# Agent attention followed by a maxout feed-forward on one core: w_out loaded after the first hosted group's keys and values, and the first batch's linear product copied out of PSUM by VectorE

## The chip, the core and the metric

The kernel runs on 1 core of one Trainium2 chip. The metric is the device time of one execution in microseconds (us). Each kernel is run several times, and the median is given. A profiled execution gives the trace, in which every instruction has its start and its duration. The engines are named PE (TensorE), DVE (VectorE), ACT (ScalarE), POOL (GpSimd) and SP (SyncE, which here only issues DMAs).

## What is computed

```
scale = 1 / sqrt(128)
sm(a, b)  = softmax over the last axis of scale * (a @ b^T)
agent_v   = sm(agents, k) @ v              # per batch: 49 agents x 128
x         = sm(q, agents) @ agent_v        # per batch: 12544 rows x 128
h         = max(x @ w1, x @ w2, x @ w3)    # 768 wide
out       = h @ w_out                      # 50176 rows x 128
```

There are B = 4 batches of 12544 rows, 49 agents and 128 channels, all in float32. The three weights are 128 x 768 and w_out is 768 x 128.

## The kernel before

**Algebra.** The rows of x are mixtures of 49 agent rows, so the kernel multiplies agent_v with the weights once per batch and gets a small matrix G (tile `G`, bf16). A query tile is then worked on from its 49 exponentials e alone (tile `e_q`). The maximum over three products is written as w1's product plus a maximum of differences: x@w1 + max(0, x@(w2-w1), x@(w3-w1)). The columns of `wall` are therefore the differences w2-w1 (from C21) and w3-w1 (from C31), and behind them (from C1O) the *linear part*, w1 @ w_out, 128 columns wide. For one of the six blocks of 128 hidden columns (number FI = 3) the differences are formed in another way, and its two steps accumulate in one tile. The reciprocal of the sum of e (tile `recips`) is applied at the end, in `out_scale`.

**Ramp.** The keys and values of batch 0 are handled first, in 12 groups. SP loads keys and values (L315, tiles `st`), POOL casts the keys (L320, `k_bf`), PE transposes them (L334, `uv_ps`), DVE copies the result to SBUF (L340, `kT`), PE multiplies with the agents (L352), ACT takes exponentials (L357, `e_k`), PE multiplies them with the values (L363), and DVE adds up (L375, `Vacc`). At the end DVE normalises (L442, L443, `avT`), and PE and DVE form batch 0's G from `wall` in pieces (L456; L471, L477, L478 and L482 copy out of PSUM).

**Linear part of batch 0.** It depends on w_out, which is loaded late. `load_w_out` (L233) puts the load into SP's queue, and `prep_w_out` (L262) casts it on POOL to `wo_bf`. PE multiplies it with the transposed w1 in six steps (`prep_linear1`, L276) into the PSUM tile `o_ps`. `linear_out` (L280) copies 128 columns of that into `wall`. `linear_product` (L285) multiplies them with `avT` into another part of the same PSUM tile, and `linear_product_out` (L289) copies 256 columns into G's last columns. `out_linear` (L620) is the first reader of those.

**Steady part.** The queries are handled in 49 groups of 8 tiles of 128 rows (`q_group`, s = 0 to 48). POOL casts (L538, `q_bf`). PE transposes (L543) and DVE copies out (L549, `qT`; for group 0 ACT does it, L551); later groups use a transposing DMA instead (L558). PE forms the scores (L564) and ACT the exponentials (L570, `e_q`). Then for each of the six hidden blocks: PE forms both differences (L590, `uv_ps`), ACT applies the relu to one of them (L605, `a_sb`) and DVE takes the maximum with the other (L615, `r`). For block FI ACT does both steps (L602, L613). PE multiplies with w_out (L629, `o_ps`), DVE scales (L642, `o_sb`) and SP stores (L649). The sums of e are L578, their reciprocals L584. While the queries of one batch are handled, the keys and values of the next one are handled beside them, one group in each query group (*hosted* groups; for the first two the keys are transposed by PE, for the others by DMA, L336). At a batch border the totals are formed (L435, L445) and G of the next batch (L456, L463).

**Order of the work.** Nothing is scheduled by a compiler. Each step is entered with a key, `at(key, fn, name, needs, ring, frees)`, and `emit` sorts by the key, holding a step back until the steps that it needs are entered and its ring of PSUM buffers has a free one. The rings are "uv" with 3 buffers, "om" with 2, and "a" with 3 (this one in SBUF). Each engine then works on its own instructions in that order, and waits for others by semaphores. The keys come from tables (`KEY`, `BEGIN` and others); one query group is 6.0 long. `KEY["u0"]` is -0.804, so `last_key`, the key of batch 0's last key group, is -2.804. Loads go into a ring of 14 tiles. SP's DMAs take eight semaphores in turn, and one is issued only when the DMA eight before it has landed.

The steps of the diff were entered like this:

```
at(key, linear_out, "linear_out", [("linear", f) for f in range(NF)])   # key = 6 + KEY["a0"] + 0.01
at(key + 0.4, linear_product, "lin_b", ["linear_out"])
at(6 + KEY["a1"] + 0.01, linear_product_out, "lin_c", ["lin_b", ("normalise", 0)])
at(last_key - 29.85, load_w_out)
at(last_key - 3.24, prep_w_out)
```

Among SP's loads this places w_out behind the load of query group 0 and ahead of the keys and values of hosted group 0.

Of the kernel before, what the change touches and what calls it, by code (L numbers as in the profile page):

```python
# [11 lines left out]
AF = mybir.ActivationFunctionType  # L12
# [4 lines left out]
def kernel(  # L17
# [18 lines left out]
    nc = tc.nc  # L36
    B, N, C = q.shape
# [121 lines left out]
    def at(key, fn, name=None, needs=(), ring=None, frees=()):  # L159

        ops.append((key, len(ops), fn, name, needs, ring, frees))
# [76 lines left out]
    C21, C31, C1O = 0, Dff, 2 * Dff  # L240
    wall = const.tile([P, 2 * Dff + 3 * C], BF16, name="wall")
    nc.vector.memset(wall[:, C1O:], 0.0)
    WC = 2 * Dff + 2 * C
# [26 lines left out]
    linear = {}  # L270
# [4 lines left out]
    def prep_linear1(f):  # L275
        nc.tensor.matmul(linear["t"][:, :C], w1T[:, f, :], wo_bf[:, f, :], start=(f == 0),  # L276
                         stop=(f == NF - 1))

    def linear_out():
        nc.scalar.activation(wall[:, C1O + C:C1O + 2 * C], linear["t"][:, :C], AF.Copy)  # L280

    def linear_product():
        for h in range(2):
# [2 lines left out]
                             start=False, stop=True, skip_group_check=True)  # L286

    def linear_product_out():
        nc.scalar.activation(G[0][:, C1O:WC], linear["t"][:, C:3 * C], AF.Copy)  # L289

    def keep_busy(times):
        t = small_tile("m_ps")
# [4 lines left out]
    G = {}  # L297
# [410 lines left out]
    def ramp():  # L708

        at(KEY["lin1"] - 6, linear_tile, "linear", ["lin_a"], "om", ["lin_c"])  # L710
        keys = sorted(KEY[f"oc1{f}"] for f in range(NF))
        for f, key in enumerate(keys):
            at(key - 6, lambda f=f: prep_linear1(f), ("linear", f), ["linear"])
        key = 6 + KEY["a0"] + 0.01
        at(key, linear_out, "linear_out", [("linear", f) for f in range(NF)])
        at(key + 0.4, linear_product, "lin_b", ["linear_out"])
        at(6 + KEY["a1"] + 0.01, linear_product_out, "lin_c", ["lin_b", ("normalise", 0)])

# [1 line left out]
    last_key = KEY["u0"] - 2  # L722
# [3 lines left out]
    at(first_key - 6.5, load_weights)  # L726
    at(first_key + 30.2, prep_weights)
    at(first_key + 37.1, prep_linear0, "lin_a", (), "om", ["lin_a"])
    at(last_key - 29.85, load_w_out)
    at(last_key - 3.24, prep_w_out)  # L730
    fillers = []
    for g, n in enumerate(first_sizes):
        k_group(0, sum(first_sizes[:g]), n, first_key + 6.0 * g, None)
# [16 lines left out]
    for s in range(NQ):  # L750
        q_group(s)
    ramp()

    with tc.manual_schedule():
# [31 lines left out]
```

## Time and profile before

| | |
|---|---|
| time, median of 5 runs | 461.55 us (461.52 to 461.67) |
| the profiled execution: its own time | 461.54 us |
| its span, first to last instruction | 459.7 us |
| TensorE clock granted | 0.999 of full speed |
| busy PE / DVE / ACT / POOL | 95% / 87% / 87% / 37% of the span |

A time in the trace is counted from the span's start. A line of the timeline gives start, duration, engine, source line, operation, the tiles (written <- read), their shape, and in brackets how long the engine had stood idle before and what ended that. A line of the chain gives start, duration and what the chain passed through. "issue" there is time in which the engine waited for nothing that the profile shows, and a q behind an engine's name stands for its sequencer, the part that reads instructions and waits for semaphores.

### The profile page before, as it was taken

The page shows a single profiled execution, that of the slowest core. Times are in us where ns is not written, and L with a number is a line of the kernel's source. Part 1 is how long each engine was busy: PE and PEld are TensorE (multiplying, and loading weights), DVE is VectorE, ACT ScalarE, POOL GpSimd, SP SyncE. Part 2 cuts the span into 40 slices and gives each one's busy share as a digit, 9 for nine tenths or more (in the row PEclk, how much of TensorE's full clock was granted, in tenths as well). Part 3 has the DMA queues.
Part 4 walks back from the last instruction along what each step waited for, and adds up shares of the span by engine and source line. Part 5 has one row for each costly group of instructions (what it writes and reads, how often), then busy time and mean ns, then how long its engine had stood idle before and what let it go on. Part 6 is the DMA issues. An engine that isn't in the chain of part 4 may idle for free.

```text
span 459.7 us, 13330 instructions
## 1 busy us (share of the span) xinstructions
PE 436.7 (95%) x5462; PEld 274.0 (60%) x5462; DVE 401.7 (87%) x510; ACT 397.8 (87%) x464; POOL 171.3 (37%) x179
## 2 busy tenths in 40 slices
PE   2598999999999999999999999999999999999996
PEld 2465456666656666666656666666656555555554
DVE  3256899999989999999989999999988999999995
ACT  3365989899899899898999998998999999998993
POOL 2234964644362535535272446354150100100000
PEclk9999999999999999999999999999999999999999
DMA  8999999999999899997998999996856556553212
GB/s 315 409 411 390 356 343 354 334 344 266 305 305 310 282 282 311 298 270 226 243 358 298 279 295 334 278 269 193 179 115 186 159 169 179 159 140 96 89 69 116
DMA packets 82632, 118.53 MB, mean 258 GB/s; under 512 B 56391, under 2 KB 57867, under 8 KB 82571
## 3 DMA queue, kind: packets, MB, share of 16 engines
q1 hardware_dynamic: 82368, 117.59, 84.7%
q8 instruction: 42, 0.69, 0.6%
q14 instruction: 19, 0.16, 0.1%
q10 hardware_dynamic: 203, 0.10, 0.1%
HBM read 78.74 MB, written 25.69 MB: 227 GB/s over the span
## 4 chain that ended last, share of the span: by engine, by line
PE 81%; DMA 9%; DVE 3%; ACT 3%; issue 1%; SPq 1%; POOL 0%; ACTq 0%; POOLq 0%; DVEq 0%
PE uv_ps L590 35%; PE o_ps L629 30%; DMA st<-in_k_dram 7%; PE o_ps L620 6%; PE m_ps L543 4%; PE m_ps L564 3%; DVE r L615 3%; ACT a_sb L605 2%; DMA st<-in_v_dram 2%; PE m_ps L363 2%; PE m_ps L352 1%; PE m_ps L578 1%; SPq L315 1%; ACT e_q L570 0%; ACT G L463 0%
## 5 line engine op out<-in xcount | busy, mean ns | idle before, releaser
L615 DVE TENSOR_TENSOR r<-uv_ps,a_sb 128x1024 bf16<-128x1024 f32 x245 | 297.4, 1220 | 16.5 <-PE uv_ps L590 7.8
L605 ACT ACTIVATE a_sb<-uv_ps 128x1024 bf16<-128x1024 f32 x245 | 241.2, 1028 | 13.7 <-PE uv_ps L590 12.3
L590 PE MATMUL uv_ps<-e_q,G 49*128 49x512 bf16 (+3 forms) x1248 | 186.7, 368 | 1.8 <-ACT a_sb L605 0.4
L629 PE MATMUL o_ps<-wo_bf,r 128*128 128x128 bf16 x2352 | 175.4, 220 | 0.0
L629 PEld LDWEIGHTS <-r 128*128 128x128 bf16 x2352 | 137.7, 98 | 40.6 <-issue 39.0
L590 PEld LDWEIGHTS <-G 49*128 49x128 bf16 x1248 | 58.1, 93 | 64.0 <-issue 32.1
L382 POOL TENSOR_TENSOR Eacc<-Eacc,e_k 128x441 f32<-128x441 f32 (+1 forms) x30 | 30.4, 1015 | 124.5 <-ACT e_k L357 124.5
L642 DVE TENSOR_TENSOR o_sb<-o_ps,recips 128x512 f32<-128x512 f32 x97 | 66.8, 689 | 8.4 <-PE o_ps L629 5.6
L538 POOL CAST q_bf<-st 128x1024 bf16<-128x1024 f32 x49 | 50.9, 1040 | 62.2 <-DMA qT<-q_bf 59.2
L613 ACT ACTIVATE r<-uv_ps 128x1024 bf16<-128x1024 f32 x49 | 50.2, 1024 | 19.6 <-PE uv_ps L590 19.3
L320 POOL CAST k_bf<-st 128x1152 bf16<-128x1152 f32 (+2 forms) x45 | 50.2, 1117 | 29.2 <-DMA st<-in_k_dram 27.4
L602 ACT ACTIVATE uv_ps<-uv_ps 128x1024 f32<-128x1024 f32 x49 | 49.7, 1013 | 0.3
L620 PE MATMUL o_ps<-G,e_q 128*128 128x256 bf16 x196 | 38.0, 276 | 0.0
L327 POOL CAST v_bf<-st 128x1152 bf16<-128x1152 f32 (+1 forms) x33 | 37.4, 1134 | 0.6 <-PE m_ps L352 0.3
L570 ACT ACTIVATE e_q<-m_ps 128x512 bf16<-128x512 f32 x49 | 29.9, 610 | 0.5 <-PE m_ps L564 0.5
L325 ACT ACTIVATE v_bf<-st 128x1152 bf16<-128x1152 f32 (+1 forms) x12 | 12.9, 1074 | 14.2 <-DMA st<-in_v_dram 14.1
L340 DVE COPY kT<-uv_ps 128x1152 bf16<-128x1152 bf16 (+1 forms) x14 | 9.9, 710 | 15.2 <-PE uv_ps L334 15.2
L620 PEld LDWEIGHTS <-e_q 128*128 128x128 bf16 x196 | 12.5, 97 | 17.9 <-issue 17.3
L543 PEld LDWEIGHTS <-q_bf 128*128 128x128 bf16 x264 | 14.9, 98 | 13.0 <-issue 10.6
L549 DVE COPY qT<-m_ps 128x1024 bf16<-128x1024 bf16 x32 | 21.8, 681 | 0.1
L543 PE MATMUL m_ps<-ident,q_bf 128*128 128x128 bf16 x264 | 20.4, 220 | 0.3 <-POOL q_bf L538 0.3
L334 PE MATMUL uv_ps<-ident,k_bf 128*128 128x128 bf16 x116 | 11.2, 255 | 9.4 <-POOL k_bf L320 8.4
(75 smaller groups left out, 236.6 us busy)
## 6 DMA issues: line engine op xcount, KB each, us to landing
st<-in_q_dram SPq DMA_DIRECT2D x46, 512.0 KB, 4.8
out_dram<-o_sb SPq DMA_DIRECT2D x46, 512.0 KB, 3.7
st<-in_k_dram SPq DMA_DIRECT2D x40, 576.0 KB, 6.8
st<-in_v_dram SPq DMA_DIRECT2D x40, 576.0 KB, 8.3
st<-in_k_dram SPq DMA_DIRECT2D x3, 512.0 KB, 7.2
st<-in_v_dram SPq DMA_DIRECT2D x3, 512.0 KB, 7.9
wst<-in_moe_w_dram SPq DMA_DIRECT2D x3, 384.0 KB, 10.4
st<-in_q_dram SPq DMA_DIRECT2D x2, 384.0 KB, 4.8
```

Source lines behind the costliest of these rows:

```text
L320: nc.gpsimd.tensor_copy(out=d["kb"][:, :n, :], in_=d["k"][:, :n, :])
L327: nc.gpsimd.tensor_copy(out=d["vb"][:, :n, :], in_=d["v"][:, :n, :])
L538: nc.gpsimd.tensor_copy(out=d["qb"], in_=d["q"])
L543: nc.tensor.transpose(t[:, j * P:(j + 1) * P], d["qb"][:, j, :], ident)
L590: nc.tensor.matmul(t[:, h, j0 * P:j1 * P], G[b][h * H:h * H + A, col + f * P:col + (f + 1) * P], d["e"][h * H:h * H + A, j0 * P:j1 * P], s ...
L602: nc.scalar.activation(u, u, AF.Relu)
L605: nc.scalar.activation(a_sb[f], u, AF.Relu)
L613: nc.scalar.activation(r, v_ps[f], AF.Relu)
L615: nc.vector.tensor_tensor(out=r, in0=v_ps[f], in1=a_sb[f], op=ALU.max)
L620: nc.tensor.matmul(t[:, i * 2 * C:(i + 1) * 2 * C], d["e"][:, jj * P:(jj + 1) * P], G[batch[jj]][:, C1O:C1O + 2 * C], start=(i == 0), stop ...
L629: nc.tensor.matmul(t[:, c:c + C], r_sb[f][:, h, jj * P:(jj + 1) * P], wo_bf[:, f, :], start=False, stop=True, skip_group_check=True)
L642: nc.vector.tensor_tensor(out=d["out"][:, j:j + m, :], in0=d["o", o].rearrange("p (j c) -> p j c", c=C), in1=d["r"][:, j:j + m].unsqueeze( ...
```

## The change

`load_w_out` gets the key -24.55, just behind the load of hosted group 0 (-24.6). In SP's queue w_out now stands behind that group's keys and values and ahead of query group 1. `prep_w_out` gets the key -6.084 instead of -6.044. On POOL the cast of w_out now stands ahead of the cast of query group 1 instead of behind it. `linear_out` and `linear_product_out` are copies by DVE instead of ACT, and the second has another key: on DVE the first stands behind the last two `r` of query group 0 and ahead of a reciprocal (L584) and an addition to `Vacc` (L375), the second behind these two and ahead of the first `r` of query group 1. PE's order is the same.

```diff
     def linear_out():
-        nc.scalar.activation(wall[:, C1O + C:C1O + 2 * C], linear["t"][:, :C], AF.Copy)
+        nc.vector.tensor_copy(out=wall[:, C1O + C:C1O + 2 * C], in_=linear["t"][:, :C])
...
     def linear_product_out():
-        nc.scalar.activation(G[0][:, C1O:WC], linear["t"][:, C:3 * C], AF.Copy)
+        nc.vector.tensor_copy(out=G[0][:, C1O:WC], in_=linear["t"][:, C:3 * C])
...
-        at(6 + KEY["a1"] + 0.01, linear_product_out, "lin_c", ["lin_b", ("normalise", 0)])
+        at(6 + KEY["ka"] + 0.01, linear_product_out, "lin_c", ["lin_b", ("normalise", 0)])
...
-    at(last_key - 29.85, load_w_out)
-    at(last_key - 3.24, prep_w_out)
+    at(-24.55, load_w_out)
+    at(last_key - 3.28, prep_w_out)
```

## The prediction, made before the changed kernel ran

> **What bounds the kernel now.** I read the page's chain first: by engine it is almost all TensorE (PE), the rest a DMA part and small pieces of VectorE (DVE) and ScalarE (ACT). Then the chain of waits cut to the first 70 us, where everything that the diff touches runs.
>
> ```profile
> PE 81%; DMA 9%; DVE 3%; ACT 3%; issue 1%; SPq 1%; POOL 0%; ACTq 0%; POOLq 0%; DVEq 0%
> 35.22 8.38 DMA st<-in_k_dram
> 43.75 1.16 POOL k_bf L320
> 44.95 0.68 PE uv_ps L334 x9
> ...
> 54.31 1.02 ACT a_sb L605
> 55.34 0.18 ACT wall L280
> 55.52 0.04 issue
> 55.56 0.30 PE o_ps L285 x2
> ...
> 61.33 0.04 issue
> 61.37 0.39 PE uv_ps L590 x2
> ```
>
> Until 43.6 us the chain is loads; the last is the keys of batch 1's group 0, cast by GpSimd (POOL) and turned by PE. It passes both moved evacuations (L280; L289 follows 1 us later) and leaves ACT at 61.37. From there PE runs without a gap up to the batch borders, and since PE's instructions keep their order, what the first 61 us gain or lose is carried to the end. So the sum is made there. Next, the engines by time:
>
> ```profile
> 43.75 1.15 POOL L320 CAST k_bf<-st 128x1152 bf16<-128x1152 f32 x1 [2.02 <-DMA st<-in_k_dram]
> 45.18 1.15 POOL L327 CAST v_bf<-st 128x1152 bf16<-128x1152 f32 x1 [0.28 <-DMA st<-in_v_dram]
> 46.41 1.04 POOL L538 CAST q_bf<-st 128x1024 bf16<-128x1024 f32 x1
> 47.39 0.83 POOL L262 CAST wo_bf<-wo_st 128x768 bf16<-128x768 f32 x1
> ...
> 51.88 3.49 DVE L615 TENSOR_TENSOR r<-uv_ps,a_sb 128x1024 bf16<-128x1024 f32 x3
> 56.29 0.41 ACT L289 ACTIVATE G<-o_ps 128x256 bf16<-128x256 f32 x1
> 58.46 1.02 ACT L613 ACTIVATE r<-uv_ps 128x1024 bf16<-128x1024 f32 x1 [0.85 <-PE uv_ps L590]
> ```
>
> POOL stands 2.02 us before k_bf, and PE 0.91 before L334 because of it. DVE is full when L280's input is ready.
>
> **Part 1: w_out behind group 0's keys and values.** SP issues load n when load n-8 has landed, so the issues (1.43 us apart per 576 KB) show the landings. Group 0's query load lands at 40.65 (it releases the issue at 40.70), w_out at 41.85 (issued 33.75, 8.1 to landing), the keys at 43.60, the values at 45.03, group 1's query (q1) at 46.36. Bytes and order beyond these three loads do not change: keys 1.25 earlier at 42.35, values at 43.8, w_out at 45.03, q1 still at 46.36.
>
> POOL: k_bf runs 42.50 to 43.65. PE is free at 44.04 (44.95 less 0.91), so L334 starts 0.91 earlier and the rest of the 1.25 is lost to PE's own work. What is late next: the first hidden product (u0, L590) waits for DVE's second 512-column copy of G (L478, ends 44.90), so it starts at 44.95 instead of 45.56, 0.61 earlier. Its a_sb and the fourth L590 pair, which waits for that a_sb, move by 0.61 too, and PE would reach the turn of q1 (L543, now 47.83) at 47.22. But q1's cast cannot start before 46.41, as now: it ends at 47.45, and the turn comes at 47.50 (0.05 from POOL's end to PE, as at 44.90 to 44.95). **Gain 0.33**, not 1.25. The steps behind it follow one another with no slack of their own: qT (L549), the r at 49.10, the turn at 50.38 that waits for that r, the a_sb and e_q up to 54.31, the three r up to 55.37. All move by 0.33.
>
> The cast of w_out now stands before q1's on POOL: 45.1 to 45.9, in the time in which POOL waits for q1. That cover is 0.45; beyond it each us that w_out lands later is a us on q1's cast. Its reader on PE (L276, 52.80) does not notice. On SP the load passes two others and waits one lane later; the issues before and after stand as they are. The next key and value casts (48.16, 49.31) wait for loads landing at 47.73 and 49.17, and L334's second turn waits for the r anyway: nothing.
>
> **Part 2: two evacuations from ACT to DVE.** L280 on DVE (128x128, fp32 to bf16) is not in the trace. Nearest rows: CAST 128x512 0.69 and 128x256 0.42 (L477, L471), so about 0.29; bounds 0.20 (COPY 128x49, L378) and 0.42. L289 is 128x256: 0.42 against ACT's 0.41. On the path: the third r ends at 55.04 (55.37 less 0.33) and stands before L280 in the queue; L276 is done by then. L280 ends about 55.30 and L285 starts at 55.35 instead of 55.56: of the 0.33 only 0.21 is left here. Behind L280 wait the reciprocal and Vacc (0.36 together, no early readers). L289 waits for L285's end (55.65) and ends at 56.10, before L620 (56.57). Behind it stands the r at 56.29, whose input PE gives at 55.97: 0.1 late at most, with 0.25 of slack before its PE reader.
>
> ACT loses 0.18 and 0.27 of its row (starts 55.23 to 55.39 and 56.29 to 56.56). L602 then waits for PE alone: 56.18 to 57.20, where it ended at 57.62 and held back the L590 pair at 57.67 by 0.12. That pair comes at 57.34, so 0.33 stands again.
>
> [...]
>
> **Part 3: the stall on ACT, and how the instruction count moves it.** L613 at 58.46 starts 0.40 after the end of its matmul pair (58.06). At the second border a DVE r shows the same, with its sequencer already released:
>
> ```profile
> 239.29 0.02 DVEq L615
> 239.31 0.40 issue
> 239.70 1.24 DVE r L615
> ...
> 350.65 0.02 DVEq L615
> 350.68 0.04 issue
> 350.72 1.24 DVE r L615
> q14 instruction: 19, 0.16, 0.1%
> ```
>
> The last line is a DMA queue: packets, MB, share. 0.40 against 0.04. Counted in the trace, semaphore instructions included, the stalled ones are ACT's 64th, DVE's 448th (and 192nd, at 110.99, 0.35 idle), POOL's 69th (68.32, 0.42): for DVE 256 apart, and ACT's place modulo 128 is the same. About 3 us after each, queue q14 moves a packet of 8 KB. I read it as a step in the instruction supply that stops an engine's sequencer for 0.35 at each 128th instruction, and is seen only when nothing is queued behind it. In the built program ACT has one instruction less before L613 (two copies out, one semaphore wait in) and DVE two more. So the stop falls on the a_sb behind L613, under L613's 1.02 us. L613 then starts at 57.83: 58.46 less 0.33 less 0.30. The a_sb pair (1.95 long, 0.92 behind) ends at 60.70, and PE's wait at 61.37 ends at 60.74. **Gain at 61 us: 0.63.**
>
> Later stops: DVE's 192nd falls under an r instead (the six L590 at 112.86 took 0.92 where others take 0.78: 0.14 back), the 448th too (238.85 to 242.50 took 3.65 where the first border's like stretch, 137.52 to 141.01, took 3.49: 0.16 back). Against it DVE's stop at 174.9 shows for some 0.05, and ACT's at 446.47 delays an a_sb by 0.17 and the L590 pair behind L602 by 0.14. Net 0.11 back, taken as 0.12.
>
> [...]
>
> **Sum.** 0.33 + 0.30 + 0.12 = 0.75 off the profiled execution's 461.54 (span 459.7, 1.8 around it): 460.79; off the median 461.55: **460.8 us**.
>
> **Rivals.**
> *A, the stops stay where they are:* 0.33 alone, 461.2. For it: three or four events are few to count by. Against: the distances fit.
> *B, q1 is not the bound:* if q1's load landed 0.3 sooner (the slowest three of a load's 16 parts come some 1.1 after the others, and their lag moves by 0.3 at 43.3), PE's own 0.61 would pass: 0.61 + 0.30 + 0.12, 460.5. For it: that lag. Against: q1 has the same bytes before it.
> *C, slower: w_out blocks POOL.* Place: w_out's cast ahead of q1's. It lands 8.1 after issue now; the same size in wst took 10.4. Issued at 36.70 it would land at 47.1, q1's cast would end at 48.96 and the turn start 1.19 late; with 0.42 back from the stops that is 462.3, and from 10.6 on (462.5) it is slower. Against it: SP's order and equal bytes put it at 45.03.
> *D, nothing moves:* the keys' gain is eaten by u0's wait for G and L280's by DVE's queue; 461.5. Against it: 0.61 of slack at u0.
>
> **How the numbers follow.** A measurement of this kernel tells about 0.2%, 0.92 us, from no change: faster is below 460.63. The forecast 0.50, B 0.25, A 0.15, D 0.05, C 0.05. The forecast's own spread is 0.25 (0.1 for L280's bounds, the rest landing times), so some 0.16 of its half lies below 460.63; of B 0.23. Together faster 0.40, same 0.55, slower 0.05. The range goes from B less 0.2 (460.3) to A plus 0.2 (461.4).
>
> **What would show it.** Right: k_bf at about 42.5, wo_bf at 45.1 before q_bf at 46.41, L543 at 47.50, L280 on DVE at about 55.0, L613 at 57.8 without the extra 0.35, the L590 behind the a_sb pair at 60.7, no 0.40 "issue" near 239. Wrong: q_bf later than 46.5 (C), L543 near 47.2 (B), L613 still 0.4 behind its matmuls (A), or a shift after 61 us that grows or shrinks by more than 0.2 outside those stops.

## The result, and the profile after

The changed kernel takes **460.68 us** (median of 23 runs, 460.53 to 461.10) where the kernel before takes 461.58 (43 runs in the same comparison, 461.32 to 462.01). The ratio is 0.998, with a 95% interval of 0.9974 to 0.9985: 0.90 us less. The interval excludes 1, though 460.68 is just above the 460.63 that I had set as the border of a measurable gain. The forecast was 460.8, from a sum of 0.75.

The profiled execution of after is one of its slowest, 461.08 us with a span of 459.295, so the two traces differ by 0.45 only. I return to that below. First the chain of waits of after, in the ramp and up to PE's wait at 61 us (start, duration, what the chain passed through):

```profile
37.49 9.34 DMA st<-in_q_dram
...
46.88 1.05 POOL q_bf L538
...
47.98 0.64 PE m_ps L543 x8
...
55.50 0.21 DVE wall L280
...
55.75 0.30 PE o_ps L285 x2
...
58.22 0.39 ACT r L613
...
59.14 1.94 ACT a_sb L605 x2
...
61.13 0.39 PE uv_ps L590 x2
```

The last load on the chain is now q1's, not the keys of group 0, and L280 stands on it as a DVE piece. PE's pair behind the a_sb starts at 61.13 where it was 61.37, although the turn of q1 starts later than before (47.98 for 47.83). The next lines are POOL's part of the timeline, and then DVE's and ACT's around the moved copies (start, duration, engine, line, operation, tiles, shapes, idle time before it and its releaser):

```profile
43.02 1.15 POOL L320 CAST k_bf<-st 128x1152 bf16<-128x1152 f32 x1 [1.18 <-PE m_ps L294]
...
45.56 0.83 POOL L262 CAST wo_bf<-wo_st 128x768 bf16<-128x768 f32 x1
46.88 1.04 POOL L538 CAST q_bf<-st 128x1024 bf16<-128x1024 f32 x1 [0.49 <-DMA st<-in_q_dram]
```

```profile
55.41 0.28 DVE L280 CAST wall<-o_ps 128x128 bf16<-128x128 f32 x1
56.09 0.42 DVE L289 CAST G<-o_ps 128x256 bf16<-128x256 f32 x1 [0.20 <-PE o_ps L285]
56.63 1.01 ACT L602 ACTIVATE uv_ps<-uv_ps 128x1024 f32<-128x1024 f32 x1 [0.22 <-PE uv_ps L590]
58.22 1.02 ACT L613 ACTIVATE r<-uv_ps 128x1024 bf16<-128x1024 f32 x1 [0.58 <-PE uv_ps L590]
```

POOL has done w_out's cast 0.49 before q1 lands, so that cast is hidden, and q1's cast waits for its DMA. L602 now waits for PE (0.22) and no longer for ACT's own copies. L613's bracket says 0.58 where it said 0.85. Its sequencer is released at 58.16, so 0.06 is left of the 0.37 that lay between the release (58.09) and the start before.

The later places where I expected a shift, in the chain of after (L590 at the second hidden stretch, the second border, and the last groups):

```profile
112.62 0.77 PE uv_ps L590 x6
...
238.46 0.39 PE uv_ps L590 x2
238.85 0.78 PE o_ps L629 x12
...
447.55 0.88 PE uv_ps L590 x6
```

In the chain of before, the six L590 ahead of L613 and the six at 112 read:

```profile
57.39 0.90 PE uv_ps L590 x6
...
112.86 0.92 PE uv_ps L590 x6
```

The six at 112 take 0.77 now, the 0.40 of "issue" at the border is gone, and the six at 447 took 0.75 before (448.11 0.75): two gains and a loss, each where it was forecast.

### The profile page after: what moved, and what is told of

The parts are those of the page before. It is cut to its first block, busy times and chain, and to the rows that moved or that the text cites. A ratio compares the mean times of both kernels' runs of the same rounds, so it can differ in the third digit from the quotient of the medians.

```text
span 459.3 us, 13331 instructions
## 1 busy us (share of the span) xinstructions
PE 437.0 (95%) x5462; PEld 274.7 (60%) x5462; DVE 402.2 (88%) x512; ACT 397.0 (86%) x462; POOL 171.5 (37%) x179
## 4 chain that ended last, share of the span: by engine, by line
PE 81%; DMA 10%; DVE 4%; ACT 3%; issue 1%; POOL 0%; ACTq 0%; SPq 0%; DVEq 0%
PE uv_ps L590 34%; PE o_ps L629 30%; PE o_ps L620 6%; DMA st<-in_k_dram 5%; PE m_ps L543 4%; DVE r L615 4%; PE m_ps L564 3%; DMA st<-in_v_dram 2%; DMA st<-in_q_dram 2%; ACT a_sb L605 2%; PE m_ps L363 2%; PE m_ps L352 1%; DMA ag_st<-in_agents_dram 1%; PE m_ps L578 1%; ACT G L463 0%
## 5 line engine op out<-in xcount | busy, mean ns | idle before, releaser
L590 PE MATMUL uv_ps<-e_q,G 49*128 49x512 bf16 (+3 forms) x1248 | 186.3, 368 | 1.7 <-DVE G L478 0.2
L590 PEld LDWEIGHTS <-G 49*128 49x128 bf16 x1248 | 58.1, 93 | 63.8 <-issue 31.3
L613 ACT ACTIVATE r<-uv_ps 128x1024 bf16<-128x1024 f32 x49 | 50.2, 1024 | 19.3 <-PE uv_ps L590 19.1
L602 ACT ACTIVATE uv_ps<-uv_ps 128x1024 f32<-128x1024 f32 x49 | 49.6, 1012 | 0.4 <-PE uv_ps L590 0.2
L543 PEld LDWEIGHTS <-q_bf 128*128 128x128 bf16 x264 | 14.8, 98 | 13.6 <-issue 11.1
L543 PE MATMUL m_ps<-ident,q_bf 128*128 128x128 bf16 x264 | 20.4, 220 | 0.7 <-POOL q_bf L538 0.7
L564 PE MATMUL m_ps<-qT,agT 128*64 128x512 bf16 (+3 forms) x104 | 19.9, 388 | 0.0
```

The source lines that it names most:

```text
L543: nc.tensor.transpose(t[:, j * P:(j + 1) * P], d["qb"][:, j, :], ident)
L590: nc.tensor.matmul(t[:, h, j0 * P:j1 * P], G[b][h * H:h * H + A, col + f * P:col + (f + 1) * P], d["e"][h * H:h * H + A, j0 * P:j1 * P], s ...
L602: nc.scalar.activation(u, u, AF.Relu)
L613: nc.scalar.activation(r, v_ps[f], AF.Relu)
```

## The experiments

**The base.** All further kernels start from one in which the 47 DMA transposes are plain copies. Its edit:

```
-  nc.sync.dma_start_transpose(out=d["kT"][:, :n, :], ...      # L336
+  nc.sync.dma_start(out=d["kT"][:, :n, :], ...
-  nc.sync.dma_start_transpose(out=d["qT"], ...                # L558
+  nc.sync.dma_start(out=d["qT"], ...
```

> Before, with its 47 DMA transposes (L336, L558: k tiles from batch 1's group 2 on, q tiles of the late groups) replaced by plain DMA copies of the same tiles, so that those tiles go on untransposed; every compute engine's instructions are the same and in the same order. All further kernels here are built on this base. Both theories: the first 61 us as in before (L543 47.83, L613 0.40 behind its matmuls, PE's pair at 61.37), 0.40 before the L615 at 239; 461.6, if no copy stood on the path, else less by what the transposes cost there.

Measured: 461.79 us against 461.70 of before, ratio 1.0002 (0.9994 to 1.0011). Its span is 459.749 where before's is 459.747, and it keeps the landmarks within 0.04 (k_bf 43.76, L543 47.85, L613 58.50). The transposes are off the path, and the base can stand for before. Before itself was measured anew beside each set of kernels (461.58, 461.70 and 461.78), so each difference to it is taken within one set.

**After, on this base.**

> After, on the base of plain copies. The same steps as after against before: L613 within 0.1 of its matmuls, no 0.40 near 239, ACT's 832nd late at 446; 0.9 below the base, the medians' difference, of which I forecast 0.75. If q1's load lands at 46.4 in this profile, L543 is at 47.50; if it lands at 46.8 as in after's profile, at 48.0.

Measured: 460.71, 0.99 below before and 1.08 below the base, ratio to before 0.998 (0.9971 to 0.9988). q1's cast started at 46.69, between the two cases I had named, and L543 at 47.79.

**The loads alone.**

```
 linear_out, linear_product_out, "lin_c": as before (ACT, key a1)
-    at(last_key - 29.85, load_w_out)
-    at(last_key - 3.24, prep_w_out)
+    at(-24.55, load_w_out)
+    at(last_key - 3.28, prep_w_out)
```

> The load and cast of w_out as in after, both evacuations (L280, L289) still on ACT, on the base of plain copies. Theory (q1's cast bounds the ramp, stops fall on each 128th instruction): L334 near 44.1, L543 near 47.50 (0.05 behind q1's cast) where before has 47.83; ACT's 64th instruction is L613 as in before, so it starts 0.35 to 0.40 behind its matmuls again; the L590 pair behind the a_sb's comes 0.33 earlier, at about 61.04; nothing changes later; 0.33 below the base. Rival D (the keys' gain is eaten on the way): within 0.1 of the base. Rival B (q1 not the bound): L543 at 47.2, 0.6 below. If all of after's gain is the loads': 0.9 below.

Measured: 461.47, 0.23 below before (ratio 0.9993, 0.9985 to 1.0002) and 0.32 below the base. The sign is not settled by the first interval; the size is near the 0.33 of the theory. Its chain:

```profile
46.86 1.05 POOL q_bf L538
...
47.96 0.63 PE m_ps L543 x8
```

L543 follows q1's cast at once, but at 47.96, not at the expected 47.50, since q1 landed late; in this one profile nothing is gained (span 459.83, the base 459.75). L613 starts at 58.60, 0.37 behind its sequencer's release (58.23), as in before. Behind L543 nothing is gained either: the span less L543's start is 411.87, in the base 411.90.

**The copies alone.**

```
 load_w_out, prep_w_out: as before
+        nc.vector.tensor_copy(out=wall[:, C1O + C:C1O + 2 * C], ...)   # L280
+        nc.vector.tensor_copy(out=G[0][:, C1O:WC], ...)                # L289
+        at(6 + KEY["ka"] + 0.01, linear_product_out, ...)
```

> L280 and L289 on DVE as in after, the load and cast of w_out where before has them, on the base of plain copies. Theory of the stops: no gain up to L543 (47.83 as before); L280 waits for DVE's third r and ends 0.1 to 0.15 later than on ACT, L285 about 55.70; L602 then waits for PE and takes most of this back; L613 starts within 0.1 of its matmuls, since ACT's 64th instruction is now the a_sb behind it; pair at 61 us about 0.3 earlier; second border without the 0.40 before L615 (0.16 back), DVE's stop at 111 gone (0.14 back), ACT's 832nd delays an a_sb at 446 (0.14 lost). Sum about 0.45 below the base. Rival A (the extra 0.35 belongs to L613's place, not to its number): as the base, or 0.1 slower with L280's delay.

Measured: 461.19, ratio 0.9989 (0.998 to 0.9998), 0.51 below before, 0.60 below the base (expected 0.45). Chain and ACT timeline:

```profile
44.06 1.16 POOL k_bf L320
...
55.92 0.30 PE o_ps L285 x2
```

```profile
58.40 1.02 ACT L613 ACTIVATE r<-uv_ps 128x1024 bf16<-128x1024 f32 x1 [0.58 <-PE uv_ps L590]
```

In this execution the keys landed 0.30 later than in the base's, which puts everything 0.30 late up to DVE's queue. L285 is 0.35 late (55.92 for 55.57), so DVE's queue costs 0.05, less than the 0.10 to 0.15 I expected. L613 is 0.10 *early*, without its extra time. Behind L543 the span is 411.30, 0.60 less than the base. So this part of the change brings some two thirds of the gain. Rival A is out.

**One idle ACT instruction more in after.** If the instruction count decides, one more ACT instruction that does nothing useful must bring the stop back.

```
+    spare = const.tile([P, 2], FP32, name="spare")
+    nc.scalar.activation(spare[:, 1:2], ones[:, 0:1], AF.Copy)     # in the preparation, once
```

> After on the base of plain copies, with one ACT instruction more in the preparation (one element of ones copied to a spare tile that nobody reads), so that L613 is ACT's 64th instruction again and the 832nd falls on a semaphore instruction as in before. DVE's stay as in after. Theory (stops at each 128th instruction): L613 starts 0.35 to 0.40 behind its matmuls where the base's after has 0.06, everything behind it some 0.3 later; at 446 the a_sb starts on its event and 0.13 comes back; 460.9 where this base's after had 460.71. Rival (the stop went away because of the loads, or because L280 and L289 run on DVE): L613 within 0.1 of its matmuls, 460.7.

ACT in the timeline of the base's after, and of this kernel:

```profile
58.04 1.02 ACT L613 ACTIVATE r<-uv_ps 128x1024 bf16<-128x1024 f32 x1 [0.58 <-PE uv_ps L590]
```

```profile
58.41 1.02 ACT L613 ACTIVATE r<-uv_ps 128x1024 bf16<-128x1024 f32 x1 [0.91 <-PE uv_ps L590]
```

The sequencer is released at 58.02, and L613 starts 0.39 later; in the base's after it was 57.98 and 0.06. The matmul pair behind the a_sb starts at 61.31 for 60.94. The loss of 0.13 at 446 does not occur. Everything behind L543 takes 411.56 for 411.31, 0.25 more: 0.32 at 61 us, less 0.13 at 446, and 0.07 that grows evenly over the run and has no place. The time is 461.28, ratio 0.9988 (0.998 to 0.9997): 0.50 below before, where the base's after is 0.99 below. The sign and the places are those of the theory; 460.9 was expected, and the medians differ by 0.49 instead of 0.2. That surplus is not explained by this trace.

**Three idle instructions more in before.**

```
+    spare = const.tile([P, 2], FP32, name="spare")
+    nc.vector.memset(spare[:, 0:1], 0.0)                           # twice
+    nc.scalar.activation(spare[:, 1:2], ones[:, 0:1], AF.Copy)     # once
```

> Before on the base of plain copies, with three instructions more in the preparation that do nothing for the output (one ACT, two DVE, on a spare tile): more work, other counts. DVE's 192nd and 448th then fall where after has them; ACT's 64th is the semaphore instruction ahead of L613, reached while L602 runs. Theory: L613 within 0.1 of its matmuls (some 0.35 gained at 61 us), the steps of 0.15 at 111 and 0.16 at 239 appear as in the kernel with the copies alone; ACT's 704th, an L613 near 378 us, starts 0.35 late, which costs between 0 and 0.35. Sum 0.35 to 0.7 below the base: 461.05 to 461.4, faster than before although it does more. Rival (count means nothing): 461.75.

Measured: 461.35, 0.43 below before (ratio 0.999, 0.9982 to 0.9999): faster, with more to do. ACT in its timeline, at 58 us and at 378 us:

```profile
58.59 1.02 ACT L613 ACTIVATE r<-uv_ps 128x1024 bf16<-128x1024 f32 x1 [0.54 <-PE uv_ps L590]
...
378.19 1.02 ACT L613 ACTIVATE r<-uv_ps 128x1024 bf16<-128x1024 f32 x1 [0.28 <-PE uv_ps L590]
```

At 58 us the extra time is gone (release 58.53, start 58.59), with the copies still on ACT. At 378 us, at ACT's 704th instruction, it has appeared: release 377.85, start 378.19, where the base has 377.99 and 378.05. There it costs PE 0.03 only. The steps at 111 (0.14) and 239 (0.16) are as in the kernels with the copies on DVE. At 61 us, counted from L543, the idle instructions gain 0.32 (13.23 to PE's pair, the base 13.55), the copies alone 0.40 (13.15): what the copies bring there is the count for the most part, and 0.08 the move itself.

**w_out behind q1 too.** This asks whether q1 is the bound of after.

```
-    at(-24.55, load_w_out)
-    at(last_key - 3.28, prep_w_out)
+    at(-19.95, load_w_out)
+    at(last_key - 3.24, prep_w_out)
```

> After on the base of plain copies, with w_out issued behind q1's load too (q1 takes w_out's place, w_out q1's), and cast behind q1's cast. Theory (q1's cast is what bounds the ramp in after): q1 lands about 1.3 earlier, at 45.1 to 45.4, its cast starts behind v_bf's at 45.1 to 45.5, L543 waits for PE's own work alone and starts near 47.2 where after has 47.5 to 48.0, w_out cast from 46.5 or so, long before L276 at 52; 0.3 to 0.6 below after: 460.1 to 460.4. Rival (the bound is elsewhere on PE or DVE, as in D): L543 not before 47.5 and 460.7. Slower, if w_out's cast now stands before the next key cast at 48.2: 461.0 or more.

POOL in its timeline, and the chain:

```profile
45.36 1.04 POOL L538 CAST q_bf<-st 128x1024 bf16<-128x1024 f32 x1
46.63 0.83 POOL L262 CAST wo_bf<-wo_st 128x768 bf16<-128x768 f32 x1 [0.23 <-DMA wo_st<-in_moe_w_out_dram]
```

```profile
43.64 0.69 DVE G L477
44.33 0.61 DVE G L478
...
60.42 0.39 PE uv_ps L590 x2
```

q1's cast runs 1.3 earlier, L543 starts at 47.26, and the chain's ramp consists of DVE's copies of G: q1 is not on it. The time is 460.47, ratio 0.9973 (0.9962 to 0.9983): 1.31 below before, where the base's after is 0.99 below; the 0.32 is in the expected range, the time itself 0.07 above it. So q1 was the bound of after, and with it away PE's own 47.2 appears, the price that rival B had.

**The same, with one idle ACT instruction late in the kernel.**

```
+    spare = const.tile([P, 1], FP32, name="spare")
+    at(6.0 * 45 + KEY["a0"] + 0.02, lambda: nc.scalar.activation(spare, ones[:, 0:1], AF.Copy))
```

> The kernel with w_out behind q1, and one idle ACT instruction (ones to a spare tile) entered in group 45, behind ACT's 704th instruction and before its 832nd: the 832nd is then a semaphore instruction that is reached under a running a_sb. Theory: as the kernel without it up to 446 us, then no loss of 0.13 at the end: 0.1 below it, 460.0 to 460.3. Rival: the stop at the 832nd does not depend on the number, or the idle instruction costs its own 0.2 us on ACT: as the kernel without it, or slower by up to 0.2.

Its chain near the end, where the kernel without it has "446.90 0.88 PE uv_ps L590 x6":

```profile
447.01 0.76 PE uv_ps L590 x6
```

The loss of 0.12 is gone. The time is **460.31**, ratio 0.9969 (0.9958 to 0.9981), 1.47 below before and the fastest here; the 0.16 to the kernel without it is near the noise of seven runs, but the trace shows the step itself.

**After twice more, one execution each.**

> The base's after again, one execution, to see what its executions differ in. Theory (q1's landing bounds the ramp, and it comes at another time in each execution): L543 starts 1.10 behind the start of q1's cast whatever that is (between 46.3 and 46.9), and the span is L543's start plus 411.3; in an execution of the median time (span 458.9) q1's cast starts at 46.5. Rival (executions differ elsewhere): L543 at 47.8 as before, and the difference in the rest.

> As the one before it: L543 1.10 behind the start of q1's cast, span 411.3 plus L543's start; rival: the spans differ by something behind L543.

Measured: spans 459.237 and 459.283, q1's casts at 46.67 and 46.69, L543 at 47.77 and 47.79, again 1.10 behind. An execution with q1's cast at 46.5 was not among them. The rest is 411.47 and 411.49, not 411.31: 0.16 more, which grows evenly from 100 to 450 us and has no place in the chain. So the landing explains part of what executions differ in; the even drift stays open.

## Why the prediction was right

Each step is best read against L543's start, since the executions differ in when loads land.

| kernel | k_bf starts | q1's cast starts | L543 starts | span less L543 |
|---|---|---|---|---|
| before | 43.75 | 46.41 | 47.83 | 411.92 |
| base | 43.76 | 46.40 | 47.85 | 411.90 |
| copies alone | 44.06 | 46.71 | 48.15 | 411.30 |
| before with three idle | 44.19 | 46.83 | 48.27 | 411.35 |
| loads alone | 42.26 | 46.86 | 47.96 | 411.87 |
| after | 43.02 | 46.88 | 47.98 | 411.32 |
| after, base | 42.84 | 46.69 | 47.79 | 411.31 |
| after with one idle | 42.40 | 46.75 | 47.84 | 411.56 |
| w_out behind q1 | 42.22 | 45.36 | 47.26 | 411.40 |

**Part 1, the loads: right, with a landing time that is no constant.** In the four kernels with the old order L543 starts 4.08 to 4.09 behind k_bf's start; in those with w_out between values and q1 it starts 1.09 to 1.10 behind q1's cast. So the bound passed from the keys to q1, as the step said. The forecast took q1's landing (46.36) from one execution, and such an early landing was not met again with the new order. SP's queue shows the landing, since SP issues the eighth load after q1 then (at 46.42 in before, 0.06 behind it): with the old order q1 landed at 46.36, 46.35, 46.66 and 46.78 (before, base, copies alone, before with three idle), with the new one between 46.63 and 46.83 in all six profiles. Whether the new order itself costs q1 a tenth, or the first two executions were early ones, four profiles against six do not settle. After's own profile has q1 at the late end. That is why L543 stands 0.15 later in it than before's, instead of 0.33 earlier, and why the traces differ by 0.45 and the medians by 0.90. No profile shows the 0.33; it rests on the medians, in which the loads alone are worth 0.23 (against before) to 0.32 (against the base). w_out's cast was hidden by 0.49, forecast 0.45; rival C did not come, since w_out landed 8.7 after its issue.

**The signs that the prediction named.** w_out's cast ahead of q1's, L613 without the extra time and no 0.40 near 239 came. k_bf started between 42.24 and 43.02 (42.5 was named). L543 at 47.50, L613 at 57.8 and the pair at 60.7 came in no profile of after: 47.77 to 47.98, 58.02 to 58.22 and 60.93 to 61.13, all late with q1. And one sign of being wrong did come: q1's cast later than 46.5, which the prediction had given to rival C. It is not C, since POOL had done w_out's cast 0.49 before q1 landed; a late landing of q1 by itself had no place among the signs. How the loads' share of the median came out near the forecast in spite of this is not shown by any profile; luck may have a part in it.

**Part 2, the copies: right, with the price of DVE's queue too high.** L280 took 0.28 (forecast 0.29) and L289 0.42 (0.42). DVE's queue costs L285 0.05 against L543, where the forecast had 0.12: L280 starts 0.09 before the `r` ahead of it has ended (55.41 and 55.50), and so adds 0.21 to the chain, not 0.26. L602, which waits for PE alone, wins back the 0.12 of the forecast (the six L590 at 57.39 took 0.90, those at 112 take 0.77 now), so 0.07 to 0.08 more are left than the sum held. The copies out of PSUM themselves took as long on DVE as on ACT: 0.28 in after against ACT's 0.27 in before for L280, 0.42 against 0.41 for L289.

**Part 3, the stops: right in count and place, too small in size.** From L543 to PE's pair at 61 us before took 13.54 (47.83 to 61.37), after 13.15: 0.39, forecast 0.30. The stop itself is 0.31 of that (0.37 to 0.06 at L613), the rest is what part 2 left. Later: 0.15 for 0.14 at 111, 0.17 for 0.16 at 239, 0.13 lost for 0.14 at 446. The loss at 174.9 was seen (0.08 in the r near 176) but is gone by 187, so it is no term of the sum. Later net 0.19 instead of 0.12. Behind L543 this makes 0.58 where the trace has 0.60 and the forecast had 0.42.

**The sum.** Behind L543 0.60 was gained where 0.42 was forecast. Of the 0.90 between the medians that leaves 0.30 for the loads, forecast 0.33. The terms that were mis-sized are the one at 61 us (0.39 for 0.30) and, next, the later net (0.19 for 0.12). Rival A needed L613 to keep its 0.35; it loses it in the kernel with idle instructions as in the one with other copies, and gets it back from one idle instruction. Rival D falls to the copies alone (0.60 below the base) and to w_out behind q1, where L543 starts at 47.26, so that u0's wait does not eat the keys' gain. Two small readings of the prediction were off: w_out landed at 41.90, not at 41.85, in before, and POOL's 69th instruction does not stand at 64 modulo 128 like the other stops, so it says nothing for the spacing. With a spread of 0.25 taken as a standard deviation, 0.12 of the forecast's half lay below 460.63, not 0.16.

**On the count of the stops.** The visible stops on ACT stand, over all kernels, at its 64th instruction (before, the base, the loads alone, after with one idle), its 704th (before with three idle) and its 832nd (after, the copies alone). They are 640 and 128 apart. From the release to the start 0.37 passes at the 64th in before (58.09 to 58.46), 0.34 at the 704th (377.85 to 378.19) and 0.34 at the 832nd in after (445.70 to 446.04), where L613 in after, the 63rd there, takes 0.06. DVE's visible ones in before, the 192nd and the 448th, stand at the same place modulo 128. So a spacing of 128 fits all five; that each 128th instruction stops its engine is not shown (DVE's 576th in before starts 0.10 behind the one ahead of it, 303.25 and 303.35). In after ACT's 64th is a semaphore instruction that starts at 58.60, 0.38 behind L613, which runs to 59.24. The a_sb behind it starts 0.92 behind L613's start, as in before: no time is lost there. That the supply of instructions is what stops the engine is my reading, and no run shows it. The packets on queue q14 do not settle it: in before one of 8 KB starts 3.4 behind ACT's 64th (at 61.86), 2.6 and 3.2 behind DVE's two (113.61 and 242.87), but in after one starts only 0.65 behind ACT's 832nd (446.69). What the runs show is the count: one idle instruction brings the stop back to L613 (0.39 for 0.06), three take it from there (0.06 for 0.37), and one late in the kernel ends the loss of 0.12 near 447.

## What to carry to other kernels

Where an edit is worth 0.2% of the time, as here, it also changes the number of instructions on an engine, and that alone can move the time as much as the edit itself (0.43 for three idle instructions, 0.51 for the two copies). Count the instructions of each engine, semaphore instructions included, look for instructions that start 0.3 to 0.4 after their release at equal spacing, and try an idle instruction before believing that a change of engine paid. When a load is moved, ask which load is last afterwards: what is won is the distance to that one, and a landing time read from one execution carries its own few tenths of a microsecond (q1 landed between 46.63 and 46.83 in six profiles of the new order, and the forecast had 46.36).

## What was not expected of the hardware

The loads land up to 0.6 us apart from execution to execution: in the three profiles of the base's after, one and the same kernel, k_bf starts at 42.84, 42.24 and 42.25, and in the four kernels with the old order between 43.75 and 44.19. This is half of the whole effect or more, and profiles taken once differ by it. The DMA records of the traces show something that goes with it. Each load lands in 16 parts. In before the last part is 0.11 behind the fourth from last in the load that lands at 19.76; one part is 1.18 behind from 22.29 on, two are over 1 behind from 36.63 on, three from 43.60 on. Ahead of each step a packet of 16 KB starts on the instruction queue q8 (19.41, 33.35 and 40.82) that takes 1.0 to 1.1 us. All twelve traces have these three packets and three steps. Where q1 stands in its place of before, the last but one of its parts lands between 45.97 and 46.29 and the last 0.25 to 0.69 behind it, so most of q1's scatter is in one part. No run moved these packets; that they are the cause is not shown.

The throughput of the DMA engines falls while w_out is on its way. In the DMA view from 8 to 48 us (40 slices of 1 us, GB/s) the base shows 363, 345 and 371 from 38 to 41 us, the base's after 340, 352 and 380 from 41 to 44 us, the kernel with w_out behind q1 367, 354 and 365 from 42 to 45 us, and most slices around them about 410. The slow stretch moves with this one load, whose packets are small (768 of 512 bytes; those of the keys and values have 4608); why it is slow was not tried.
